# Attention sums with the values stationary and 512 columns moving, on one core of Trainium2

## The chip, the core and the metric

The kernel runs on one core of a Trainium2 chip. The metric is the device time of one execution in microseconds. It is taken as the median of several runs; for the kernel before it is 2655.85 us (three runs, 2655.58 to 2656.35).

## What is computed

All data are f32. An attention without softmax is followed by a mixture of experts in which a hash of the token's id picks the expert.

```
B, S, D = 8, 2496, 256;  K = 64                  # z is (B, S, K)
scores = (1/S) * z @ z.T                          # symmetric, per batch
x = u * (max(scores, 0)**2 @ v)                   # (B, S, D)
expert = token_ids * 2654435761 % 8               # per token
out[token] = max(x[token] @ w1[expert], 0) @ w2[expert]   # w1 256 x 1024, w2 1024 x 256
```

## The kernel before, in words

**Tiles and groups.** The 2496 tokens of a batch are 20 tiles (T): 19 of 128 and a last one, TM, of 64. Five groups (NG) of four tiles (G) are the queries; each group sums over all 20 tiles. The squared scores are symmetric, so for a group g only the tiles of later groups and its own are computed (`fresh`); those of earlier groups are obtained by turning blocks that were made before. All of the order is written out by hand; each engine executes its own instructions in exactly that order.

**Scores** (`scores`, line 206). One matmul per tile gives 128 keys by 512 queries in one bank of `mm_ps` (six banks). K is 64, so two matmuls share the array, by halves of its rows. ScalarE (ACT), and VectorE (DVE) for a few, writes the relu to a block `a` (pool `apool`, seven buffers of 4 tiles x 512). `square` (line 226) squares in place on ACT, two tiles per step of the main loop. In a group's own block only the part above the diagonal is computed, in most groups (`skipped`), and `own_turns` (line 258) turns small pieces in place.

**Turns** (`turns_of`, line 244). A block of group a with g > a is turned for group g by 16 DVE transposes, each of 32 partitions x 512, which write straight to the right quarter of a `mirror` buffer. `turn_scores` (line 283) issues some at each step, by a budget of ns; `turn_now` issues the rest where a user comes.

**Sums** (`attend`, line 333). For each tile and each of four query tiles, the 128 x 128 squares are the stationary operand and `v` (128 keys x 256) moves; the result, queries by 256, lies in two accumulators of two halves (`acc`). The last group has three whole query tiles and one of 64, which `attend_short` (line 305) sums by itself in a 64-column strip. `attend_last` adds the short tile TM, by halves of the rows.

**Gates** (`gate`, line 341). DVE multiplies `acc` by u and (1/S)^2 into `x_sb`. `place_x` (line 552) scatters each 128 rows of x to the token's slot in DRAM (`x_rows`), by an indirect DMA on GpSimd (POOL).

**Order of a group** (main loop, line 640). Two first tiles (EARLY) for half the queries, then for the other half; tiles 2 to 15, one per step; the short tile; then the scores of the next group; then the last three tiles (LATE) and the gates, half by half. After each step `square`, `turn_scores` and `between` add their work; `between` also spreads the sort of tokens by expert (`places`), the clearing of `x_rows` and the scatters. Loads of u, v and z stand on SyncE's (SP's) queue at the starts of groups.

**Experts** (`run`, line 763). Blocks of 512 slots and of 128 slots alternate. `ups` multiplies by w1 into `h_ps` and relus on ACT and DVE in turn; `down` multiplies by w2. `load_w`, `load_x` (both on SP) and `turn_x` (DVE) prepare the next blocks. Block 0 is loaded before the attention ends.

Of the kernel before, what the change touches and what calls it, by code (L numbers as in the profile page):

```python
# [24 lines left out]
def kernel(  # L25
# [10 lines left out]
    nc = tc.nc  # L36
# [29 lines left out]
    NS = -(-(NW * BLK // P + NP) // CLEAR) * CLEAR  # L66
    C = B * T
    c2 = (1.0 / S) ** 2
# [11 lines left out]
    NA = NG + 2  # L80
    apool = pool("apool", NA)
    xpool = pool("xpool", 3)

# [3 lines left out]


    slot_dram = nc.dram_tensor("slot_tokens", (P * NS,), I32)


    short = const.tile([P, T, R], F32)
    odd = const.tile([R, D], F32)
# [4 lines left out]
    nc.gpsimd.memset(short[R:P, TM, :], 0.0)  # L98
# [24 lines left out]
    zn, zT, v_sb, u_sb, x_sb, made, mirror, to_square, to_turn, gated = {}, {}, {}, {}, {}, {}, {}, [], [], []  # L123
# [24 lines left out]
    def load_v(b):  # L148
        v_sb[b] = vpool.tile([P, T, D], F32, name="v_sb")
        for g in range(NG):  # L150
            tiles_io(vf, b, group(g), v_sb[b][:, g * G:, :], False, nc.sync, twice=True)
# [21 lines left out]

    def whole(g):

        return range(G if g < NG - 1 else G - 1)

# [15 lines left out]
    def skipped(b, g, t):  # L193

        if t // G != g or b == 0 and not fine(g):
            return 0
        return (t % G if fine(g) else t % G // 2 * 2) * P

    def fine(g):


        return g > 1
# [3 lines left out]
    def scores(b, g):  # L206

        n = sum(width(t) for t in group(g))
        for k, t in enumerate(fresh(b, g)):
            lo = skipped(b, g, t)  # L210
# [15 lines left out]
    def square(n):  # L226
        for b, g, t in to_square[:n]:
            a = made[b, g, t // G][:, t % G, :]
            m = len(whole(g)) * P
            lo = skipped(b, g, t)  # L230
            pairs = [(a[:, lo:m], a[:, lo:m])] if lo < m else []
            if m < G * P:
                pairs.append((short[0:width(t), t, :], a[0:width(t), ds(m, R)]))
            for o, x in pairs:
                nc.scalar.square(o, x)  # L235
            if t % G == G - 1 and (t // G > g or b or fine(g)):
                turns = turns_of(b, g, t // G) if t // G > g else own_turns(b, g)
                to_turn.extend((n, (b, g, t // G), f) for n, f in turns)

                to_turn.sort(key=lambda e: min(e[1][2] - g, 2 if fine(g) else 1))  # L240
        del to_square[:n]


    def turns_of(b, a, g):

        def turn(r, c, m):
            if (b, a, g) not in mirror:
                mirror[b, a, g] = mirrors.pop(0)
            nc.vector.transpose(  # L249
# [586 lines left out]
```

## Time and profile before

| | before |
|---|---|
| median of three runs | 2655.85 us |
| profiled execution | 2659.45 us |
| its span, first to last instruction | 2657.6 us |
| TensorE busy | 2645.2 us (100%) |
| VectorE, ScalarE, GpSimd busy | 1394.4, 598.1, 495.9 us |
| attention sums, `acc` line 338, matmul instructions | 3472 + 2304 |
| first matmul of the experts starts | 1537.85 us |
| DMA | 274.44 MB |

The page shows one profiled execution. Engines are PE (TensorE's matmuls), PEld (its weight loads, which run beside PE), DVE, ACT, POOL and SP (SPq is its issuing of DMAs). An f32 matmul appears as two instructions. The ends of matmuls are modelled, so the interval from one start to the next tells TensorE's pace better than the duration. A group's line reads: line, engine, operation, out<-in, shapes, count | busy us, mean ns of one | idle time of the engine before it and what ended it. A timeline's line reads: start us, length us, engine, line, operation, count [idle before <- what released it]. L338 is line 338 of the kernel.

### The profile page before, as it was taken

Reading aid. Unit: us, or ns where it says so; the run is one execution under the profiler, and the core shown is the slowest. Engines: PE = TensorE matmul, PEld = TensorE weight load, DVE = VectorE, ACT = ScalarE, POOL = GpSimd, SP = SyncE. Lnnn points to the kernel's source line nnn. Section 1 sums busy time; section 2 is a strip of 40 time slices with the busy share of each in tenths; the row PEclk is TensorE's granted clock in tenths of the full one; section 3 lists DMA queues with packets and bytes.
Section 4 is the critical chain, followed back from the end, with each engine's and each line's share of the span. In section 5 each row is a group of like instructions: output and inputs, shape, how many; then the busy total and the mean of one; then the engine's idle time right before and its main releaser. Section 6 shows DMA issues by size and latency. Waiting matters only on the chain.

```text
span 2657.6 us, 32524 instructions
## 1 busy us (share of the span) xinstructions
PE 2645.2 (100%) x12054; PEld 2073.0 (78%) x12054; DVE 1394.4 (52%) x2907; ACT 598.1 (23%) x1304; POOL 495.9 (19%) x512
## 2 busy tenths in 40 slices
PE   9999999999999999999999999999999999999999
PEld 7787888888888888888878867777777777777777
DVE  7976887878878877887878811111111111111111
ACT  5115214223233133123142111111111111111111
POOL 1322122212221222222201111111111111111112
PEclk9999999999999999999999999999999999999999
DMA  8612212202210221122101276666666666666663
GB/s 294 202 32 71 37 32 70 51 18 70 51 59 29 51 71 37 34 69 52 33 16 32 63 182 166 158 159 153 156 158 156 155 156 164 165 165 163 165 157 84
DMA packets 306288, 274.44 MB, mean 103 GB/s; under 512 B 179116, under 2 KB 269117, under 8 KB 306128
## 3 DMA queue, kind: packets, MB, share of 16 engines
q1 hardware_dynamic: 285392, 231.25, 34.8%
q0 software_dynamic: 20736, 41.10, 4.8%
q8 instruction: 96, 1.57, 0.3%
q14 instruction: 64, 0.52, 0.1%
HBM read 208.91 MB, written 64.79 MB: 103 GB/s over the span
## 4 chain that ended last, share of the span: by engine, by line
PE 55%; issue 37%; POOL 6%; DVE 2%; POOLq 0%; DMA 0%; SPq 0%; ACT 0%
PE acc L338 45%; PE s_ps L213 7%; POOL out_dram L757 6%; PE acc L330 1%; PE q_ps L310 1%; DVE m L249 1%; POOLq L757 0%; PE warm L569 0%; POOL x_rows L555 0%; DMA v_sb<-x_rows 0%; DVE x_sb L347 0%; DMA x_rows<-x_sb,slot_i 0%; DVE slot L527 0%; DVE per_e L491 0%; SPq L614 0%
## 5 line engine op out<-in xcount | busy, mean ns | idle before, releaser
L249 DVE STREAM_TRANSPOSE m<-a 32x512 f32<-32x512 f32 (+1 forms) x1280 | 865.1, 676 | 21.5 <-ACT a L235 0.9
L338 PE MATMUL acc<-v_sb,a 128*128 128x256 f32 x3472 | 766.9, 381 | 2.2 <-issue 2.0
L338 PEld LDWEIGHTS acc<-v_sb,a 128*128 128x128 f32 x3472 | 656.9, 190 | 100.4 <-issue 10.0
L739 DVE TENSOR_SCALAR hT<-h_ps 128x512 f32<-128x512 f32 x161 | 111.4, 692 | 946.2 <-PE h_ps L733 924.2
L733 PE MATMUL h_ps<-v_sb,m 128*128 128x128 f32 (+1 forms) x2080 | 567.7, 431 | 1.4 <-PEq L797 1.4
L745 PE MATMUL o_ps<-m,hT 128*128 128x256 f32 x2576 | 566.3, 379 | 0.0
L745 PEld LDWEIGHTS o_ps<-m,hT 128*128 128x128 f32 x2576 | 486.9, 190 | 77.6 <-issue 14.3
L338 PE MATMUL acc<-v_sb,m 128*128 128x256 f32 x2304 | 504.6, 380 | 2.8 <-DVE x_sb L347 2.8
L733 PEld LDWEIGHTS h_ps<-v_sb,m 128*128 128x128 f32 x2080 | 317.6, 191 | 235.5 <-issue 230.6
L338 PEld LDWEIGHTS acc<-v_sb,m 128*128 128x128 f32 x2304 | 438.8, 191 | 63.6 <-DVE x_sb L347 3.6
L221 ACT ACTIVATE a<-s_ps 128x512 f32<-128x512 f32 (+3 forms) x456 | 205.4, 592 | 855.3 <-PE s_ps L213 855.3
L555 POOL DMA_INDIRECT x_rows<-x_sb,slot_i x160 | 156.2, 976 | 1067.8 <-DVE x_sb L347 883.6
L757 POOL DMA_INDIRECT out_dram<-o_sb,idx x157 | 153.5, 977 | 918.2 <-ACT o_sb L752 910.3
L235 ACT ACTIVATE a<-a 128x512 f32<-128x512 f32 (+3 forms) x472 | 232.8, 651 | 0.0
L265 DVE STREAM_TRANSPOSE a<-a 32x128 f32<-32x128 f32 (+1 forms) x992 | 221.6, 248 | 10.2 <-issue 1.1
L213 PE MATMUL s_ps<-zT 64*128 64x512 f32 (+1 forms) x960 | 195.0, 545 | 0.3 <-ACT zT L171 0.3
L752 ACT COPY o_sb<-o_ps 128x256 f32<-128x256 f32 x161 | 59.9, 372 | 595.4 <-PE o_ps L745 595.4
L737 ACT ACTIVATE hT<-h_ps 128x512 f32<-128x512 f32 x161 | 96.1, 597 | 368.7 <-PE h_ps L733 358.1
L213 PEld LDWEIGHTS s_ps<-zT 64*128 64x128 f32 x960 | 120.3, 186 | 71.2 <-issue 41.5
L543 POOL DMA_INDIRECT slot_tokens<-token,addr x160 | 156.1, 976 | 75.2 <-issue 50.4
L347 DVE SCALAR_TENSOR_TENSOR x_sb<-acc,u_sb 128x256 f32<-128x256 f32 x152 | 57.8, 420 | 194.7 <-PE acc L338 194.5
L633 DVE STREAM_TRANSPOSE v_sb<-v_sb 128x1024 f32<-128x1024 f32 (+1 forms) x65 | 53.9, 829 | 3.5 <-DMA v_sb<-x_rows 3.5
(101 smaller groups left out, 293.6 us busy)
## 6 DMA issues: line engine op xcount, KB each, us to landing
m<-in_moe_w_dram SPq DMA_DIRECT2D x260, 256.0 KB
m<-in_moe_w_dram SPq DMA_DIRECT2D x65, 1024.0 KB
x_rows<-zero SPq DMA_DIRECT2D x10, 2176.0 KB
v_sb<-in_v_dram SPq DMA_DIRECT2D x32, 512.0 KB
u_sb<-in_u_dram SPq DMA_DIRECT2D x32, 512.0 KB
v_sb<-x_rows SPq DMA_DIRECT2D x128, 128.0 KB
zn<-in_z_dram SPq DMA_DIRECT2D x28, 304.0 KB
v_sb<-x_rows SPq DMA_DIRECT2D x132, 32.0 KB
```

Source lines behind the costliest of these rows:

```text
L213: nc.tensor.matmul(ps[:, lo:n], zT[b][h, ts(t, P)], zT[b][h, ds(g * G * P + lo, n - lo)], start=True, stop=True)
L221: nc.scalar.activation(a, ps[:, lo:n], AF.Relu)
L235: nc.scalar.square(o, x)
L249: nc.vector.transpose(mirror[b, a, g][ts(c, Q)].rearrange("p t s q -> p (t s) q")[:, 0:m, ts(r, Q)], made[b, a, g][ts(r, Q)].rearrange("p ...
L265: return n * Q, lambda: nc.vector.transpose(out, in_)
L338: nc.tensor.matmul(acc[i // 2][:, i % 2, :], lhs(b, g, t, i), v_sb[b][:, t, :], start=(k == 0 and i % 2 == 0), stop=(k == TM - 1), skip_gr ...
L543: st = nc.gpsimd.indirect_dma_start(out=slot_dram[:, None], out_offset=bass.IndirectOffsetOnAxis(ap=addr[0:n, c:c + 1], axis=0), in_=token ...
L555: st = nc.gpsimd.indirect_dma_start(out=x_dram[:, :], out_offset=bass.IndirectOffsetOnAxis(ap=slot_i[0:width(c % T), c:c + 1], axis=0), in ...
L733: nc.tensor.matmul(ps[:, ts(i, n)], w1[j][:, c, ts(k * m + i, P)], xT[j][:, :, c, :], start=(c == 0), stop=(c == DP - 1))
L739: nc.vector.tensor_scalar_max(o, ps[:], 0.0)
L745: nc.tensor.matmul(ps[:], hT[j][f][:, ts(t, P)], w2[j][:, f, :], start=(f == 0), stop=(f == FP - 1))
L757: st = nc.gpsimd.indirect_dma_start(out=out[:], out_offset=bass.IndirectOffsetOnAxis(ap=rows, axis=0), in_=o, in_offset=None, bounds_check ...
```

## The change

The roles in the sums are swapped: 128 columns of v (every second one, `h::2`) are stationary and 512 squares move, so the result comes out turned, 128 columns of x by 512 queries, in one bank per half of v. The group's 448 queries of the last group move together, and `attend_short`, `short` and `odd` go. DVE turns a quarter of a block's columns on all 128 partitions at once into a `stage` buffer (pool `spool`, five); three DMAs on SP and one copy on ACT carry the quarters to the mirror. The factor 1/S moves into the square. The gate is now a DVE transpose of a bank; four DMAs take x to DRAM (`x_way`), one or two fetch it back some steps later in token order, and POOL multiplies by u. u is loaded at step 8 of its own group, v at five places of the batch before, z in group 3. `apool` has six buffers for seven. Only padding slots of `x_rows` are cleared. The own triangle is skipped in all groups. At the experts' start, `load_w` for the first partial block comes after the attention, and block 0's down comes ahead of that block's up.

```diff
-    NA = NG + 2
+    NA = NG + 1
...
+    qpool = pool("qpool", 2)
+    spool = pool("spool", 5)
...
+    x_way = [nc.dram_tensor(f"x_way_{k}", (G, NQ, Q, D), F32) for k in range(2)]
...
+    def queries(g):
+        return sum(width(t) for t in group(g))
...
+    def skipped(g, t):
+
+        return t % G * P if t // G == g else 0
...
+            a = made[b, g, t // G][:, t % G, skipped(g, t):queries(g)]
+            nc.scalar.activation(a, a, AF.Square, scale=1.0 / S)
...
     def turns_of(b, a, g):
...
+        key = b, a, g
+        def turn(c):
+            if key not in mirror:
+                mirror[key] = mirrors.pop(0)
+            stage = spool.tile([P, G * G * Q], F32, name="stage")
+            nc.vector.transpose(stage[:].rearrange("p (n q) -> p n q", q=Q),
+                                made[key][:].rearrange("p t (s q) -> p (t s) q", q=P)[:, :, ts(c, Q)])
+            for r in range(NQ):
+
+                m = len(group(g)) if r * Q < width(group(g)[-1]) else G - 1
+                o = mirror[key][ts(c, Q), 0:m, r].rearrange("p i s q -> p i (s q)")
+                x = stage[ts(r, Q), 0:m * G * Q].rearrange("p (i n) -> p i n", i=m)
+                if r == c:
+                    to_copy.append((key, lambda o=o, x=x: nc.scalar.copy(o, x)))
+                else:
+                    nc.sync.dma_start(o, x)
+        for c in range(NQ):
+            yield lambda c=c: turn(c)
...
     def turn_scores(steps):
...
+        nonlocal share
+        copy_turned(to_copy[:])
+        share += 1.2 * steps
+        own = [e for e in to_turn if e[0][1] == e[0][2]][:3]
+        others = [e for e in to_turn if e[0][1] < e[0][2]]
+        for e in own:
+            turn(e)
+        while share >= 1 and others and (mirrors or others[0][0] in mirror):
+            turn(others.pop(0))
+            share -= 1
+        share = min(share, 1)
...
+    def attend(b, g, k, acc, halves):
         t = summed(b, g)[k]
         turn_now((b, t // G, g))
-        for i in queries:
-            if i in whole(g):
-                nc.tensor.matmul(acc[i // 2][:, i % 2, :], lhs(b, g, t, i), v_sb[b][:, t, :],
-                                 start=(k == 0 and i % 2 == 0), stop=(k == TM - 1), skip_group_check=True)
+        for h in halves:
+            nc.tensor.matmul(acc[h][:, 0:queries(g)], v_sb[b][:, t, h::2], squares(b, g, t),
+                             start=(k == 0), stop=(k == TM - 1), skip_group_check=True)
...
+    def gate(b, g, h, acc):
+        n = queries(g) // Q
+        if h == 0:
+            x_q[b, g] = qpool.tile([P, G * NQ, D // NQ], F32, name="x_q")
+        x = x_q[b, g]
+        nc.vector.transpose(x[:, 0:n, h::2], acc[h][:, 0:n * Q].rearrange("p (n q) -> p n q", q=Q))
+        if h == 0:
             return
...
+        for a in range(NQ):
+            nc.sync.dma_start(o[:].rearrange("i j p d -> p (i j) d")[:, 0:n, ts(a, D // NQ)], x[ts(a, Q), 0:n])
+        m = len(whole(g))
+        def fetch():
+            nc.sync.dma_start(xs[:, 0:m], o[0:m].rearrange("i j p d -> (j p) i d"))
+            if m < G:
+                nc.sync.dma_start(xs[0:R, m], o[m, 0:R // Q].rearrange("j p d -> (j p) d"))
+            for k, t in enumerate(group(g)):
+                y = xs[0:width(t), k, :]
+                nc.gpsimd.tensor_mul(y, y, u_sb[b, g][0:width(t), k, :])
+                gated.append((b * T + t, y))
+        to_fetch.append((i + 3, fetch))
...
+    V_LOADS = [(4, 4), (1, 9), (2, 9), (3, 6), (3, 12)]
...
-        if g == 2 and b + 1 < B:
+        if g == 3 and b + 1 < B:
             load_z(b + 1)
...
+            if t == 8:
+                load_u(b, g)
+            if b + 1 < B and (g, t) in V_LOADS:
+                load_v(b + 1, V_LOADS.index((g, t)))
+            attend(b, g, t, acc, range(2))
...
+            attend(b, g, t, acc, [k])
+            gate(b, g, k, acc)
             square(2)
             turn_scores(1 if k else 0.8)
...
+            if first < i == AHEAD:
+
+                while do:
+                    do.pop(0)()
             up = ups(work[i]) if i < last else None
...
+    load_w(work[1], 1)
     load_x(work[1], 1)
```

## The prediction

> **What bounds the kernel now.** I read the busy shares by stage first, then TensorE's timeline, then the groups by shape, then the waits. By stage (columns: stretch; busy PE, PEld, DVE, ACT, POOL with counts; granted clock; DMA share; GB/s):
>
> ```profile
> core 0: us, PE busy (x) PEld busy (x) DVE busy (x) ACT busy (x) POOL busy (x), PEclk, DMA share, GB/s
> ...
> 100.00:140.00 40.00, 35.35 (x152) 28.15 (x150) 32.04 (x70) 2.88 (x8) 12.91 (x13) 0.91 0.37 73
> 175.00:365.00 190.00, 190.00 (x922) 158.26 (x923) 151.29 (x330) 54.95 (x124) 43.91 (x45) 1.00 0.18 49
> 365.00:554.00 189.00, 189.00 (x920) 157.39 (x918) 152.55 (x332) 54.05 (x122) 43.83 (x45) 1.00 0.18 49
> ```
>
> One batch takes 189.6 us (the chain of waits has the same 26.10 us piece of line 338 start at 364.62 and again at 554.23). In it TensorE is never idle, DVE is at 80%, ACT at 29%, DMA at 18%. So a lighter DVE is worth nothing by itself in seven of eight batches; only TensorE's own time counts. "Busy" could still hide slack, so I take start-to-start intervals from the timeline in the expert stage (each f32 matmul is two instructions):
>
> ```profile
> 2004.61 13.98 PE L745 MATMUL o_ps<-m,hT 128*128 128x256 f32 x64
> 2018.42 3.60 PE L733 MATMUL h_ps<-v_sb,m 128*128 128x512 f32 x8
> 2021.86 3.62 PE L745 MATMUL o_ps<-m,hT 128*128 128x256 f32 x16
> 2025.31 1.02 PE L733 MATMUL h_ps<-v_sb,m 128*128 128x512 f32 x2
> ```
>
> 256 columns: (2018.42-2004.61)/64 = 215.8 ns. 512 columns: (2021.86-2018.42)/8 = 430 ns. The wide form saves about 2 ns in 432. TensorE already streams columns without a gap, and the change leaves the number of columns nearly alone. This is the main fact of the case.
>
> The only idle TensorE time in the attention is in batch 0:
>
> ```profile
> 99.47 1.99 PE L338 MATMUL acc<-v_sb,m 128*128 128x256 f32 x8 [0.36 <-DVE x_sb L347]
> 103.94 14.04 PE L338 MATMUL acc<-v_sb,m 128*128 128x256 f32 x56 [2.48 <-DVE x_sb L347]
> ...
> 123.35 0.47 PE L338 MATMUL acc<-v_sb,a 128*128 128x256 f32 x1 [0.19 <-issue]
> 125.46 0.49 PE L338 MATMUL acc<-v_sb,a 128*128 128x256 f32 x1 [1.64 <-issue]
> 126.16 6.12 PE L338 MATMUL acc<-v_sb,a 128*128 128x256 f32 x20 [0.21 <-issue]
> ```
>
> 4.9 us in all, where the gates (line 347) stood behind turns and the sort on DVE; the clock of 0.91 over these 40 us is another 40 x 0.09 = 3.6 us. The groups that change:
>
> ```profile
> L249 DVE STREAM_TRANSPOSE m<-a 32x512 f32<-32x512 f32 x1024 | 719.1, 702 | 17.9 <-ACT a L235 0.9 <-issue 0.6
> L338 PEld LDWEIGHTS acc<-v_sb,a 128*128 128x128 f32 x3472 | 656.9, 190 | 100.4 <-issue 10.0
> L162 DVE STREAM_TRANSPOSE zT<-zn 128x512 f32<-128x512 f32 x35 | 24.1, 703 | 0.4
> ```
>
> A transpose of 128 partitions takes as long as one of 32.
>
> **The skill.** "TensorE: Matmul & The Clock Gate", section "Wait — 56ns, not 53.3ns?": warm, matmuls start N/2.4 GHz + 2.5 ns apart. With two columns' time per column of f32 that is 215.8 ns for 256, as measured, 429.2 for 512 (measured 430), and 375.8 for 448, which I use. Same page, "What's actually happening": the clock is halved or freed by windows of 3413 ns; the trace agrees in kind, since the slow stretches come just after the idle ones above. "SBUF — State Buffer", section "Door 1": lines of 16 bytes, strides up to 4 f32 cost nothing; the weights' new stride is 2, no run here shows one. "DMA: Bandwidth & Descriptors", section "Anatomy of one DMA": about 2 us fixed per DMA; it is told of GpSimd's path, and here SP's loads at 1542.5 were used at 1545.6, with eight issues between, which agrees.
>
> **Part by part.** Sums, TensorE, on the path. Before: 3472 + 2304 = 5776 instructions x 0.2158 = 1246.5 us, and the short-tile sums (line 310) from 1528.34 to line 330's start at 1532.80, 4.46 us x 8 = 35.7. After, per batch 4 groups x 19 tiles x 2 halves of 512 and 38 of 448, two instructions each: 2432 x 0.4292 + 608 x 0.3758 = 1272.3 us. Change -9.9 us. The last short tile (line 330) keeps its columns, four instructions of 512 for eight of 256: 0.
>
> Weights with stride 2: 190 ns now. If a stride doubled it, 380 still fits below the 429 ns of a matmul: 0. Only above 429 would it show, x 3040; I leave that to the tail, since the page says such a stride is free.
>
> Scores (line 213): the own triangle is now skipped in every group, 512 columns less per batch, 1536 in batch 0, 5120 in all. 39 instructions, nearly 9728 columns, took 8.25 us (775.31 to 783.56), 0.85 ns each: -4.3 us.
>
> DVE, per batch: 160 turns of 32 partitions go (865.1/8 = 108 us), 40 of 128 come (x 0.703 = 28), own turns rise by about 50 x 0.25 = 13, gates are 10 transposes of about 0.7 for 8 us of multiplies. 152 becomes about 84 of 188 us: off the path, except that the batch 0 idle should go: -4.9 - 3.6 = -8.5 us (bounds 0 and -8.5; the sort stays on DVE, but its backlog of 1280 turns is gone).
>
> What replaces the turns: per quarter-turn three 64 KB DMAs on SP and one ACT copy. SP issues take 0.30 to 0.49 us (line 614's least and middle). 120 turn DMAs x 0.49 = 59 us per batch, x out and back 26 x 0.49 = 13, z about 14, u and v 12 x 0.4 = 5: 91 of 188. The densest stretch is group 0, 1.2 quarters per step, 3.6 DMAs x 0.49 = 1.76 us against a step of 1.72, at the low price 1.1; 16 quarters have 19 steps, so SP is done in time either way. A stage buffer is held for 0.7 + 3 x 0.49 + 2 = 4.2 us, and five of them allow one quarter per 0.84 us. First use of a quarter is a group, 33 us, or at least ten steps later. Hidden behind TensorE: 0; without that cover each late quarter costs its lateness. ACT: 40 copies x 0.65 (the square's time) = 26 on top of 54: 80 of 189. POOL: 20 multiplies of 256 columns at 2.9 us/1280 = 0.6: 12 on top of 44.
>
> Moved loads: u to step 8 of its own group, v to five places, z from group 2 to 3, x by DRAM and back. All stand on SP in order, so a wait for a gate or for x's landing (about 2 us) holds the turn DMAs behind it; their ten steps cover it. The clearing of x_rows shrinks from ten DMAs of 2176 KB to pads: nothing waits on TensorE.
>
> Entry to the experts: x's longer way (gate, out 2+2, back 3, four multiplies 2.6, scatters 5 x 1.3, landing 2, load 3: about 22 us) is covered, as block 0's up (13.8) and down (13.8, now placed before the partial block's up) run first. But the next whole block's turn on DVE now stands behind the partial block's relu (0.69 + 1.24 + 0.2 = 2.1 us) and its matmuls follow at once: +2.1, or 3.8 with a half-clock window (1.7). The old order gave 13.8 us of cover. I take +3.
>
> Sum: -9.9 - 4.3 - 8.5 + 3 = -19.7 us. The profiled execution took 2659.45 (span 2657.6) and would take 2639.8; the median of the runs is 2655.85, so I forecast 2636.
>
> **The new waits, and the rivals.** On DVE the order of the built program puts, at two boundaries of each batch, a quarter-turn between the two gates of a group. The turn waits for ACT's fourth square of the next group, and gate 1 is queued behind; TensorE waits for gate 1 before its third matmul of the next group.
>
> ```profile
> 776.36 8.51 ACT L221 ACTIVATE a<-s_ps 128x512 f32<-128x512 f32 x18 [1.51 <-PE s_ps L213]
> 784.73 10.07 ACT L235 ACTIVATE a<-a 128x512 f32<-128x512 f32 x20
> ```
>
> On this clock: scores end 783.3, six matmuls of 0.75 end 787.8; relus end 784.5, squares are 0.52 apart, the fourth is done at 786.7, the turn at 787.4, gate 1 at 788.9; TensorE wants the bank at 789.5. It fits by 0.6 us. After group 0, counted from the first score: 7424 columns x 0.85 = 6.3, six matmuls of 0.86 to 11.5, bank wanted at 13.2; sixteen relus to 8.4, the fourth square done at 10.6, the turn at 11.3, gate 1 (bank complete 11.9) at 12.6: again 0.6.
>
> Rival A, slower (16%): ACT runs late there (copies ahead of the relus wait for DVE, DVE for stage buffers), so gate 1 is late by 1.6 us or more and the clock halves (1.7 more): 3.3 us at 23 boundaries (two per batch, and group 3's, where own turns stand between the gates) = 76, giving 2712. It turns the sign from 19.7/23 = 0.86 us per boundary. For: thin margin. Against: DVE and ACT half idle.
>
> Rival B (15%): batch 0's idle stays, since the sort still interleaves with gates: 2636 + 8.5 = 2644.
>
> Rival C (8%): small stalls at group starts, 0.4 us x 40 = 16, give 2652: no change to be told (0.2% is 5 us, about what a measurement of this kernel can tell).
>
> The forecast keeps 61%, own range 2628 to 2643. Faster 0.76 (forecast and B), same 0.07, slower 0.17 (A, 0.01 of C). The range runs from 2626 to 2656, where A alone is left out.
>
> **What would show it.** Right: 3040 sum instructions 429 ns apart, line 310's work gone, TensorE idle only after the partial block's up, batch period near 188 us, DVE near 45%. Wrong: TensorE waiting for a gate at group starts, half-clock windows in every batch, weight loads over 400 ns, or copies on ACT waiting for DVE ahead of the relus.

## The result, and the profile after

The kernel after takes 2676.75 us (median of four runs, 2674.95 to 2685.0); the kernel before took 2656.1 us beside it (four runs, 2655.58 to 2657.91). The ratio is 1.0083, with a 95% interval of 1.0070 to 1.0095: slower by 0.8%, against a forecast of 2636 us. The profiled execution of after is the slowest of its four, 2685.0 us with a span of 2683.3, so it is set against before's profiled 2659.45 (span 2657.6): +25.6 us.

First the busy shares of after by stage: the stretch of batch 0 that was shown of before, then batch 2, then batch 7.

```profile
core 0: us, PE busy (x) PEld busy (x) DVE busy (x) ACT busy (x) POOL busy (x), PEclk, DMA share, GB/s
100.00:140.00 40.00, 40.00 (x104) 18.29 (x103) 22.13 (x64) 15.00 (x32) 11.80 (x13) 1.00 0.57 137
391.50:584.80 193.30, 190.11 (x524) 89.81 (x522) 76.22 (x233) 78.18 (x158) 57.98 (x66) 1.00 0.47 113
1367.20:1560.00 192.80, 192.80 (x536) 92.09 (x533) 74.29 (x230) 77.85 (x158) 33.61 (x40) 1.00 0.45 107
```

In this stretch batch 0 lost its idle time. But batch 2 takes 193.3 us where before took 189.6, although VectorE (DVE) is busy for half as long, and TensorE now has 3.2 us idle. Measured from one batch's first score to the next one's, the two profiled executions differ like this:

| | before | after | change |
|---|---|---|---|
| up to the first score | 8.91 | 9.53 | +0.6 |
| batch 0 | 197.13 | 187.37 | -9.8 |
| batches 1 to 6 | 1137.7 (189.62 each) | 1170.6 | +32.9 |
| batch 7 | 194.12 | 192.60 | -1.5 |
| experts, from their first matmul | 1119.73 | 1123.22 | +3.5 |
| sum, the span | 2657.6 | 2683.3 | +25.7 |

The groups of the sums in after, by shape, and the waits of TensorE (PE) between 190 and 1550 us (us in total, times, longest):

```profile
L323 PE MATMUL acc<-a,v_sb 128*128 128x512 f32 (+1 forms) x1760 | 768.0, 593 | 0.0
L323 PE MATMUL acc<-m,v_sb 128*128 128x512 f32 (+1 forms) x1280 | 529.2, 571 | 5.5 <-DVE x_q L339 4.5
L323 PEld LDWEIGHTS acc<-a,v_sb 128*128 128x128 f32 x1760 | 343.0, 197 | 391.6 <-issue 374.7
```

```profile
PE s_ps L210 <- ACT a L218: 11.3, 8, 2.4
PE s_ps L210 <- issue: 5.1, 4, 2.0
PE acc L323 <- DVE x_q L339: 4.5, 6, 1.1
```

The sums themselves hardly wait: 1760 + 1280 = 3040 instructions, as forecast, and weights with a stride load in 197 ns (190 before). Undisturbed intervals are 0.429 us for 512 columns and 0.376 for 448. All 11.3 + 5.1 us of waiting for relus and "issue" belongs to the scores, line 210; in before no matmul of this stretch waits at all. So I looked at one boundary between groups, where scores are made. A relu is ScalarE's reading of one tile of scores, and the first one shows when ACT learns that the first scores are done. This is the boundary from group 0 to group 1 in batch 2 of before, TensorE and then ScalarE (ACT):

```profile
437.00 6.81 PE L213 MATMUL s_ps<-zT 64*128 64x512 f32 x32
```

```profile
438.06 7.52 ACT L221 ACTIVATE a<-s_ps 128x512 f32<-128x512 f32 x16 [22.49 <-PE s_ps L213]
```

And this is TensorE there in after (start us, length, operation, count, idle before):

```profile
432.97 2.74 PE L210 MATMUL s_ps<-zT 64*128 64x512 f32 x12
437.51 5.15 PE L210 MATMUL s_ps<-zT 64*128 64x512 f32 x20 [1.79 <-issue]
442.59 5.43 PE L323 MATMUL acc<-a,v_sb 128*128 128x512 f32 x12
```

and ACT at the same time:

```profile
430.12 0.51 ACT L249 COPY m<-stage 32x384 f32<-32x384 f32 x1 [1.40 <-DVE stage L241]
431.90 0.51 ACT L249 COPY m<-stage 32x384 f32<-32x384 f32 x1 [1.27 <-issue]
436.86 0.60 ACT L218 ACTIVATE a<-s_ps 128x512 f32<-128x512 f32 x1 [4.45 <-PE s_ps L210]
437.61 6.81 ACT L218 ACTIVATE a<-s_ps 128x512 f32<-128x512 f32 x15 [0.15 <-remote]
```

The first relu starts 436.86 - 432.97 = 3.89 us after the first score; in before it is 1.06 here and at the next two boundaries (0.95 for group 4; 1.48 at the start of a batch, where the first scores are mixed with the last sums). ACT was not busy: it had been idle for 4.45 us, waiting for line 210. The twelve scores filled the six banks and TensorE stopped for 1.79 us. In the trace's semaphore records, TensorE's first completion signal of this boundary stands at 436.84, 3.44 us after the start of the matmul that gives it (433.40); in before, at the same boundary, it comes 0.60 us after the start. The other held-up signals follow close behind; at this boundary in batch 1 all six stand 42 to 45 ns apart. So by their starts the scores were made in time, and what came late was the word that they were done.

From group 0 to 1 the first relu is late in each of batches 1 to 6 (4.14, 3.89, 4.51, 1.40, 4.14, 3.91 us after the score), in batch 7 it is not (1.05; the bursts of scatters there are of four and end before the boundary). From group 1 to 2 the signals are held up about 2 us into the scores; from group 3 to 4 a gate comes 1.0 to 1.3 us late. After a stop the scores go at the pace of the relus, and after five of the stops the granted clock is 0.50 for 3.4 or 6.8 us (242.9 to 246.3, for one; after the stop at 437.51 it stays at 1.00). For batches 1 to 6 this makes +43.3 us against six undisturbed batches of 187.88 us (which runs 5 and 8 below show): 35.0 in the scores (173.5 against 6 x 23.08) and 8.3 in the sums (968.65 against 6 x 160.06).

What else runs at that boundary? GpSimd (POOL) issues its scatters, x to the tokens' rows and slots to `slot_tokens`:

```profile
421.28 2.77 POOL L354 TENSOR_TENSOR x_sb<-x_sb,u_sb 128x256 f32<-128x256 f32 x4 [29.77 <-DMA m<-stage]
424.22 1.01 POOL L562 DMA_INDIRECT x_rows<-x_sb,slot_i  x1 [0.16 <-POOL x_sb L354]
...
434.42 0.98 POOL L550 DMA_INDIRECT slot_tokens<-token,addr  x1 [0.30 <-issue]
```

Nine scatters, 1.28 us apart, lie over the boundary at 432.97. In before they lay in the middle of a group, with boundaries at 437.00 and 477.71; the first and the last of its nine:

```profile
447.34 0.98 POOL L555 DMA_INDIRECT x_rows<-x_sb,slot_i  x1 [29.45 <-DVE x_sb L347]
...
457.62 0.98 POOL L543 DMA_INDIRECT slot_tokens<-token,addr  x1 [0.31 <-issue]
```

And SyncE's queue (SPq), with all its DMAs of line 251 in after (least, median, most ns) below:

```profile
406.01 2.24 SPq L346 DMA_DIRECT2D x_way<-x_q  x4
408.35 7.80 SPq L251 DMA_DIRECT2D m<-stage  x12
416.33 0.46 SPq L349 DMA_DIRECT2D x_sb<-x_way  x1
...
417.46 14.11 SPq L251 DMA_DIRECT2D m<-stage  x21
431.67 0.54 SPq L120 DMA_DIRECT2D u_sb<-in_u_dram  x1
```

```profile
L251 SPq DMA_DIRECT2D m<-stage x960: 3/599/1653, 20.6 to 1510.0; - x192
```

"Perfetto Trace Analysis", section "DMA Instruction — HWDGE (DVE, Sync)" of the Trainium skill, says what such a slice is: waiting for the descriptor generator, using it and pushing semaphores, not the movement of data. So 0.599 us is what a DMA of 64 KB costs SP's queue. At 3 x 1.2 = 3.6 of them per step that is 2.16 us, and a step takes 1.72: SP falls behind in groups 0 and 1, where it is issuing nine us of every ten in their second halves. x's way back, behind the turns, starts only at 416.33, 16.6 us ahead of the boundary (23.4 us in run 5 below, which has no turn DMAs), and its four products and the scatters follow from there. u leaves at 431.67, 1.3 us ahead of the boundary (22.4 us in run 5).

Three things thus meet at the boundary: the moved loads (u here, u and v at the next boundaries), the scatters, and the turn DMAs of SP. The experiments take them apart.

### The profile page after: what moved, and what is told of

Read it like the earlier page. It is cut to its first block, busy times and chain, and to the rows that moved or that the text cites. A ratio compares the mean times of both kernels' runs of the same rounds, so it can differ in the third digit from the quotient of the medians.

```text
span 2683.3 us, 28098 instructions
## 1 busy us (share of the span) xinstructions
PE 2652.4 (99%) x8854; PEld 1534.3 (57%) x8854; DVE 795.7 (30%) x2147; ACT 785.0 (29%) x1592; POOL 608.9 (23%) x671
## 5 line engine op out<-in xcount | busy, mean ns | idle before, releaser
L323 PE MATMUL acc<-a,v_sb 128*128 128x512 f32 (+1 forms) x1760 | 768.0, 593 | 0.0
L323 PEld LDWEIGHTS acc<-a,v_sb 128*128 128x128 f32 x1760 | 343.0, 197 | 391.6 <-issue 374.7
L323 PE MATMUL acc<-m,v_sb 128*128 128x512 f32 (+1 forms) x1280 | 529.2, 571 | 5.5 <-DVE x_q L339 4.5
L323 PEld LDWEIGHTS acc<-m,v_sb 128*128 128x128 f32 x1280 | 250.5, 196 | 279.8 <-issue 267.7
L354 POOL TENSOR_TENSOR x_sb<-x_sb,u_sb 128x256 f32<-128x256 f32 (+1 forms) x160 | 111.1, 723 | 989.0 <-DMA x_sb<-x_way 766.1
L262 DVE STREAM_TRANSPOSE a<-a 32x64 f32<-32x64 f32 (+3 forms) x1408 | 298.8, 241 | 20.0 <-ACT a L226 6.4
L249 ACT COPY m<-stage 32x512 f32<-32x512 f32 (+1 forms) x320 | 189.6, 593 | 300.9 <-DVE stage L241 139.7
L241 DVE STREAM_TRANSPOSE stage<-a 128x512 f32<-128x512 f32 x320 | 218.0, 700 | 200.8 <-DMA m<-stage 179.5
L226 ACT ACTIVATE a<-a 128x512 f32<-128x512 f32 (+1 forms) x480 | 236.9, 564 | 2.1
L210 PE MATMUL s_ps<-zT 64*128 64x512 f32 (+2 forms) x960 | 207.6, 555 | 16.7 <-ACT a L218 11.3
```

The lines of the kernel that those rows point to most:

```text
L210: nc.tensor.matmul(ps[:, lo:n], zT[b][h, ts(t, P)], zT[b][h, ds(g * G * P + lo, n - lo)], start=True, stop=True)
L226: nc.scalar.activation(a, a, AF.Square, scale=1.0 / S)
L241: nc.vector.transpose(stage[:].rearrange("p (n q) -> p n q", q=Q), made[key][:].rearrange("p t (s q) -> p (t s) q", q=P)[:, :, ts(c, Q)])
L249: to_copy.append((key, lambda o=o, x=x: nc.scalar.copy(o, x)))
L262: return lambda: nc.vector.transpose(out, in_)
L323: nc.tensor.matmul(acc[h][:, 0:queries(g)], v_sb[b][:, t, h::2], squares(b, g, t), start=(k == 0), stop=(k == TM - 1), skip_group_check=True)
```

## Experiments

The theories are named in the expectations as they stood then. Each ratio is against before's runs on the same chip.

### Run 1: the loads earlier

```diff
-    V_LOADS = [(4, 4), (1, 9), (2, 9), (3, 6), (3, 12)]
+    V_LOADS = [(4, 4), (1, 3), (2, 3), (3, 3), (3, 5)]
...
-            if t == 8:
+            if t == 2:
                 load_u(b, g)
```

> The changed kernel, with u loaded at step 2 of its group instead of step 8, and v's tiles at steps 3 and 5 instead of 9, 6 and 12. Theory (collision): SyncE issues a turn DMA every 0.60 us, falls behind, and issues u and v so late that they are in flight during the next group's scores; together with GpSimd's indirect DMAs they hold up TensorE's completion signals, so relus and gates start 1.5 to 3.5 us late. Then the first relu comes 1.06 us after the first score at every boundary, the batch period falls from about 194.5 to 190 us, and the time from about 2676 to 2650 us. Rival (order of ScalarE and VectorE: copies and turns ahead of the relus): no change, 2672 to 2680. Rival (the turn DMAs' 512-byte packets themselves hold up the signals): no change or worse.

Measured: 2691.91 us (2690.05 to 2697.55), ratio 1.013 (1.0116 to 1.0145). The loads were no longer at the scores, but the relus came late at both boundaries, 3.6 to 4.5 us after the first score from group 0 to 1 and 1.6 to 4.8 us from group 1 to 2, and batch 2 took 196.99 us. The turn DMAs were now issued up to 446.7, with the boundary at 435.2 and a burst of nine scatters from 425.7 to 436.8. The theory that the loads do it falls.

### Run 2: no scatters in batches 1 to 6

All rows of `x_rows` are cleared, and the scatters of x and of slots in batches 1 to 6 are left out, so most of the experts' input is missing.

```diff
-        c = NW * BLK // P + k * -(-NP // CLEAR)
-        n = min(NS - c, -(-NP // CLEAR))
+        n = -(-NS // CLEAR)
+        c = k * n
+        n = min(NS - c, n)
...
-        st = nc.gpsimd.indirect_dma_start(
+        if not 0 < c // T < 7:
+            st = nc.gpsimd.indirect_dma_start(
...
         c, x = gated.pop(0)
+        if 0 < c // T < 7:
+            return
```

> The changed kernel, leaving out GpSimd's indirect DMAs (the scatter of x and of the slot numbers) for batches 1 to 6, and clearing all of x_rows in batches 0 and 1 instead; so the experts get no rows of these batches. The loads of u and v stay where they are. Read batches 2 to 6 only. Theory (collision of loads with indirect DMAs): first relus at 1.06 us, batch period 188 to 190 us. Rival (the loads alone are enough): late first relus remain, period 192 to 195. Rival (order of ScalarE and VectorE): the same, 192 to 195.

Measured: 2670.15 us (2669.62 to 2670.44), ratio 1.0042 (1.0027 to 1.0056). The total is not to be used: the larger clearing disturbs batch 0, where relus wait up to 11 us. Batch 1 still has bursts of nine, with batch 0's tokens, and there a first relu is 3.75 us behind its score. In batches 2 to 6, which have no scatters, every first relu is 1.06 us behind (0.95 for group 4) and the period is 187.88 us, with the loads and the turn DMAs still at the scores. The scatters are needed for the loss; loads and turn DMAs without them do no harm.

### Run 3: before, with its loads moved to the scores

```diff
+            if k == 0 and (b or g):
+                load_u(b, g)
+                c, h = (b, g - 1) if g else (b - 1, NG - 1)
+                if c + 1 < B:
+                    load_v(c + 1, [h])
...
-        if n + 1 < len(groups):
-            load_u(*groups[n + 1])
-        if g == 0 and b + 1 < B:
-            load_v(b + 1)
```

> The kernel before, with the loads of u and of one fifth of v moved from the middle of a group to its scores: a one-element ScalarE copy into their buffers after the first relu holds them back to that point. Nothing of the turn DMAs is in it. Theory (collision): TensorE's completion signals come late at the boundaries that have indirect DMAs, TensorE idles there, 1 to 3 us a boundary, some 20 to 40 us more than before (2675 to 2695). Rival (the turn DMAs are needed for it): within 3 us of before.

Measured: 2660.78 us (13 runs) against 2658.42, ratio 1.0008 (1.0000 to 1.0016), and every first relu as in before. A batch takes 189.83 us for 189.62. 1 MB landing during the scores is all but harmless in before too. Its scatters stayed in mid-group, so this tests the loads alone.

### Run 4: the entry to the experts in the old order

```diff
-                if k == (1 if i + 1 > AHEAD else banks[-1]) and AHEAD <= i + 1 < max(last, loads):
+                if k == (0 if i == AHEAD else 1 if i + 1 > AHEAD else banks[-1]) and AHEAD <= i + 1 < max(last, loads):
                     turn_x(work[i + 1], (i + 1) % LOADS)
```

> The changed kernel, with the turn of the next whole block's x placed ahead of the partial block's relus on VectorE instead of behind them. The step of the sum at the entry to the experts (+2.1 for the wait, +1.7 for a half-clock window) says 3 to 3.8 us less than the changed kernel. If x's way by DRAM is what is late there, no change.

Measured: 2684.85 us (six runs, 2676.19 to 2692.62), ratio 1.0099 (1.0082 to 1.0116). The attention's late signals vary from run to run by more than the entry is worth, so the trace decides. TensorE at the entry in after, and then in run 4:

```profile
1587.62 3.73 PE L742 MATMUL h_ps<-v_sb,m 128*128 128x128 f32 x32
1593.29 5.40 PE L742 MATMUL h_ps<-v_sb,m 128*128 128x512 f32 x8 [1.94 <-DVE v_sb L644]
```

```profile
1575.44 13.98 PE L754 MATMUL o_ps<-m,hT 128*128 128x256 f32 x64
1589.26 7.17 PE L742 MATMUL h_ps<-v_sb,m 128*128 128x128 f32 x40
```

The stop of 1.94 us is gone, and the eight matmuls that took 5.40 us at half clock are no longer there. The expert stage takes 1119.3 us for 1123.2: 3.9 us.

### Run 5: no turn DMAs

The three DMAs of each quarter-turn are left out, so three quarters of each mirror keep zeros.

```diff
                 if r == c:
                     to_copy.append((key, lambda o=o, x=x: nc.scalar.copy(o, x)))
-                else:
-                    nc.sync.dma_start(o, x)
...
+    for m in mirrors:
+        nc.gpsimd.memset(m[:], 0.0)
```

> The changed kernel, leaving out the three SyncE DMAs of every quarter-turn, so that only a quarter of the turned squares is right (the buffers are set to zero at the start). GpSimd's indirect DMAs and the loads stay. The second run says that the indirect DMAs are needed for the late signals, the first and third that loads at the scores are not. Theory (turn DMAs and indirect DMAs together): first relus at 0.95 to 1.06 us at every boundary of batches 1 to 6, batch period 187.9 us. Rival (the indirect DMAs with anything that this kernel added, such as x's way through DRAM): late first relus remain, period above 190 us.

Measured: 2637.69 us (one run) against 2656.36. No idle time of TensorE between 190 and 1500 us, every first relu at 1.06. A batch of run 5:

```profile
570.10:758.00 187.90, 187.90 (x523) 89.77 (x522) 75.96 (x233) 77.86 (x158) 58.02 (x65) 1.00 0.28 76
```

This is the forecast, to 2 us. All matmuls, transposes, copies and gates of the change are still in it, so the loss of 2676.75 - 2637.69 = 39 us needs the turn DMAs. It does not say how: without them SP is not behind, and the scatters too had moved away from the boundary (406.9 to 418.1, with the boundary at 423.6).

### Run 6: only the slots' scatters

x's scatters are left out in batches 1 to 6, as in run 2; the slots' stay.

```diff
         c, x = gated.pop(0)
+        if 0 < c // T < 7:
+            return
         st = nc.gpsimd.indirect_dma_start(
```

> As the second run, but with the scatter of the slot numbers (4 bytes a row) kept in all batches, and only the scatter of x (1 KB a row) left out for batches 1 to 6. If every indirect DMA of GpSimd collides with the turn DMAs, whatever it carries: late relus in batches 1 to 5, where the slot scatters run, at about half the boundaries of the changed kernel, period 189 to 193. If it is x's data that collides: period 187.9.

Measured: 2665.49 us (one run), period 187.88 us from batch 2 on. The five scatters left in a burst ended some 3 us ahead of the boundary (628.4 to 634.5, boundary 637.4), so the run says nothing on which kind is at fault. Run 14 asks it again.

### Run 7: scatters only where there are no turn DMAs

All scatters are held for groups 3 and 4, where few or no turns are sent; the edit of run 4 is in it.

```diff
-        elif i % 4 == 0 and i < SORT + 4 * C:
+        elif g > 2:
             assert next(place, None) is None
-            enter((i - SORT) // 4)
-        elif gated:
+            if entered < C and i % 5 < 3:
+                enter(entered)
+                entered += 1
+            if gated:
+                place_x()
+        elif g == 0 and gated and gated[0][0] // T < b:
             place_x()
```

> The changed kernel, with both kinds of scatter issued only in groups 3 and 4 of a batch, which have few turn DMAs, and for the last group's x in the next group 0; and with the turn of x at the entry to the experts ahead of the relus. All of the work is done. Theory (turn DMAs and indirect DMAs together): late relus only where both still meet, batch period 188 to 189 us, attention shorter by 25 to 40 us than in the changed kernel, 2638 to 2648 us in all, faster than before. Rival (indirect DMAs with any transfer): as many late signals, only elsewhere, above 2655.

Measured: 2773.6 us (2765.59 to 2779.44), ratio 1.0436 (1.0418 to 1.0453): the expectation failed. All first relus are at 1.06 us, as hoped, but now TensorE stops inside the sums. A batch of run 7, and TensorE's largest wait over the whole run:

```profile
424.30:634.40 210.10, 196.58 (x522) 92.62 (x520) 76.23 (x233) 78.03 (x158) 56.94 (x64) 0.96 0.44 104
```

```profile
PE acc L323 <- issue: 73.0, 93, 3.0
```

Bursts of 15 to 23 scatters in a row stand over most of these stops, during which the starts of neighbouring matmuls lie 0.7, 1.4 or 2.1 us apart instead of 0.376; DVE is held too. "issue" means that the profile shows nothing that TensorE waited for. There is a second way, then, in which scatters delay other engines, with no turn DMA beside them; I found no cause for it.

### Run 8: x by ACT's queue

All work is done. x's DMAs, 26 per batch, are issued by ACT, out one step and back five steps after the gate, so SP's queue keeps the turns and loads; the edit of run 4 is in it.

```diff
-        for a in range(NQ):
-            nc.sync.dma_start(o[:].rearrange("i j p d -> p (i j) d")[:, 0:n, ts(a, D // NQ)], x[ts(a, Q), 0:n])
+        def send():
+            for a in range(NQ):
+                nc.scalar.dma_start(o[:].rearrange("i j p d -> p (i j) d")[:, 0:n, ts(a, D // NQ)], x[ts(a, Q), 0:n])
...
-            nc.sync.dma_start(xs[:, 0:m], o[0:m].rearrange("i j p d -> (j p) i d"))
+            nc.scalar.dma_start(xs[:, 0:m], o[0:m].rearrange("i j p d -> (j p) i d"))
...
-        to_fetch.append((i + 3, fetch))
+        to_fetch.append((i + 1, send))
+        to_fetch.append((i + 5, fetch))
```

> The changed kernel, with x's way out to DRAM and back issued by ScalarE's DMA queue (one step after the gate, back four steps later) instead of SyncE's, so that neither a wait for the gate nor the turn DMAs stand before it, and with the turn of x at the entry to the experts ahead of the relus (3.9 us less there, by the trace of the fourth run). GpSimd's scatters then come in the middle of a group as in the kernel before, and not over its end. All of the work is done. Theory (scatters that fall on a group's boundary make TensorE's completion signals late, whatever else runs): first relus at 1.06 us, batch period 188 to 189 us, 2634 to 2645 us in all, faster than before. Rival (turn DMAs and scatters together, wherever they meet, cost TensorE time): 2655 or more.

Measured: 2635.85 us (2634.80 to 2636.67) against 2654.5, ratio 0.9929 (0.9916 to 0.9943): faster than both kernels. Batch 2 of run 8, then its boundary on TensorE, on ACT and on POOL:

```profile
382.50:570.40 187.90, 187.90 (x522) 89.75 (x520) 76.36 (x233) 78.27 (x158) 58.20 (x66) 1.00 0.50 116
```

```profile
423.84 6.60 PE L210 MATMUL s_ps<-zT 64*128 64x512 f32 x32
```

```profile
424.90 5.49 ACT L218 ACTIVATE a<-s_ps 128x512 f32<-128x512 f32 x11 [3.69 <-PE s_ps L210]
```

```profile
409.65 2.78 POOL L355 TENSOR_TENSOR x_sb<-x_sb,u_sb 128x256 f32<-128x256 f32 x4 [26.93 <-DMA x_sb<-x_way]
...
422.80 0.98 POOL L552 DMA_INDIRECT slot_tokens<-token,addr  x1 [0.31 <-issue]
```

The same operations as in after, the DMA share even higher (0.50), and no stop: 32 scores in one piece, the relu 1.06 us behind, though ACT has been idle ahead of it here too. Counted from the boundary, x's products start only 2.5 us sooner than in after (423.84 - 409.65 = 14.2 us ahead of the first score, for 432.97 - 421.28 = 11.7), but that is enough to issue the last of the nine scatters just before the first score. The turn DMAs still run over the boundary. At the next one, 464.16, a burst of nine does lie over it (454.4 to 465.7), with eight turn DMAs issued in its first half, and nothing is late there either.

### Run 9: before, with its scatters held to the scores

A small copy on POOL waits for the first relu of the next group, and the nine scatters follow it.

```diff
             to_square.append((b, g, t))
+            if k == 0 and held:
+                nc.gpsimd.tensor_copy(once_seen[:], a[0:1, 0:1])
+                release()
...
-            enter((i - 2 * T) // 4)
-        elif gated:
-            place_x()
+            held.append(lambda c=(i - 2 * T) // 4: enter(c))
+        elif len(gated) > len(later):
+            held.append(place_x)
+            later.append(0)
```

> The kernel before, with all the scatters of a group held back until the first relu of the next group: a one-element GpSimd copy of that relu's output stands ahead of them, so a burst of nine begins about 1.2 us after the first score. No turn DMA is in it. Theory (a burst at the boundary is enough): TensorE's signals come late in the scores, and TensorE idles 1.5 to 5 us at most boundaries, 50 to 150 us more than before. Rival (the turn DMAs are needed): within 5 us of before.

Measured: 2654.35 us (12 runs) against 2654.5, ratio 1.0000 (0.9991 to 1.0008). A burst of nine at the boundary is free in before. The theory that the burst is enough falls.

### Run 10: no turn DMAs, scatters held to the scores

The edit of run 9 on the kernel of run 5, so the turned data are missing again.

```diff
-            enter((i - SORT) // 4)
-        elif gated:
-            place_x()
+            held.append(lambda c=(i - SORT) // 4: enter(c))
+        elif len(gated) > len(later):
+            held.append(place_x)
+            later.append(0)
```

> As the fifth run (three SyncE DMAs of every quarter-turn left out, GpSimd's indirect DMAs kept), with the scatters held back to the first relu of the next group as in the run before this one. It has the changed kernel's burst at the boundary, and no turn DMAs. Theory (a burst at the boundary is enough): late signals and idle TensorE at most boundaries, above 2665 us. Rival (the turn DMAs are needed): 2636 to 2642 us as in the fifth run.

Measured: 2639.27 us (one run), period 187.88 us. The burst starts 2.5 us after the first score, as in run 11 below, where turn DMAs run too and it does harm. Here it does none.

### Run 11: run 8 with its scatters held to the scores

The edit of run 10, on the kernel of run 8: all work is done, only the scatters' place changes.

```diff
+            if k == 0 and held:
+                nc.gpsimd.tensor_copy(once_seen[:], a[0:1, 0:1])
+                release()
```

> The eighth run (x's way on ScalarE's DMA queue), with the scatters of a group held back to the first relu of the next group's scores as in the ninth and tenth. All of the work is done; turn DMAs and a burst of scatters now meet at the boundaries after groups 0 and 1. Theory (turn DMAs and scatters together at a boundary): late relus or idle TensorE there again, 2650 to 2680 us. Rival (it also takes x's transfers on SyncE's queue, or a SyncE that is behind): 2634 to 2642 us, as the eighth run.

Measured: 2666.51 us (2663.22 to 2669.45), ratio 1.0044 (1.0027 to 1.0061). TensorE's largest wait between 190 and 1550 us in run 11:

```profile
PE acc L326 <- DVE x_q L342: 18.6, 11, 2.8
```

The burst can start only after the first relu, so the relus are in time; the gates, a few us later, are now the late ones. The period of batch 2 is 193.1 us for 187.88. Few turn DMAs are enough: from batch 1 to 2 the burst runs from 388.5 to 399.8, only three turn DMAs are issued in it, from 398.4 on, and the second gate is late and stops TensorE for 1.69 us. Putting the burst back over a boundary with turn DMAs brings the loss back, in the version that had none: together they cost, and run 8's gain is one of place.

### Run 12: run 8 with x on SP's queue

```diff
-                nc.scalar.dma_start(o[:].rearrange("i j p d -> p (i j) d")[:, 0:n, ts(a, D // NQ)], x[ts(a, Q), 0:n])
+                nc.sync.dma_start(o[:].rearrange("i j p d -> p (i j) d")[:, 0:n, ts(a, D // NQ)], x[ts(a, Q), 0:n])
...
-            nc.scalar.dma_start(xs[:, 0:m], o[0:m].rearrange("i j p d -> (j p) i d"))
+            nc.sync.dma_start(xs[:, 0:m], o[0:m].rearrange("i j p d -> (j p) i d"))
```

> The eighth run with x's transfers back on SyncE's queue, but still sent one step after the gate and fetched four steps later, instead of at the gate and three steps later. If what the changed kernel suffers from is only the place in SyncE's order (turn DMAs that stand behind a wait for the gate): 2634 to 2645 us. If it is that SyncE has too much to issue (0.60 us a turn DMA) so that x comes back late in the group and the scatters fall on its end: 2655 to 2680 us, scatters at the boundary.

Measured: 2678.81 us (2677.22 to 2679.58), ratio 1.0086 (1.0069 to 1.0103), period of batch 2 194.4 us. TensorE over the boundary at 433.09, and the first and last of the scatters there:

```profile
433.09 4.71 PE L210 MATMUL s_ps<-zT 64*128 64x512 f32 x20
439.81 5.84 PE L210 MATMUL s_ps<-zT 64*128 64x512 f32 x12 [2.02 <-issue]
```

```profile
427.26 1.01 POOL L564 DMA_INDIRECT x_rows<-x_sb,slot_i  x1 [0.16 <-POOL x_sb L355]
...
437.45 0.98 POOL L552 DMA_INDIRECT slot_tokens<-token,addr  x1 [0.30 <-issue]
```

Fourteen turn DMAs are issued during this burst. At the next boundary, 479.96, the burst (475.2 to 486.5) meets only four, all before the first score, and nothing stops. So it is not the later steps for x that help in run 8 but the other queue: on SP, x stands behind the turns wherever the program puts it.

### Runs 13 and 14: one kind of scatter at the scores

Run 11 with the slots' scatters left out in batches 1 to 6, and run 11 with x's left out there, by the edits of run 2 (run 14 clears all rows again).

```diff
+        if not 0 < c // T < 7:
+            st = nc.gpsimd.indirect_dma_start(
```

> The eleventh run (x's way on ScalarE's DMA queue, scatters held to the next group's first relu), leaving out most scatters of slot numbers (those of tokens of batches 1 to 6), so that a burst at the boundary is four scatters of x alone; the experts then get few of the rows. If x's scatters with the turn DMAs are enough: gates and relus late at boundaries of batches 2 to 6 as in the eleventh run, period above 190.5 us. If the slot scatters are needed: 187.9 us.

```diff
         c, x = gated.pop(0)
+        if 0 < c // T < 7:
+            return
```

> The eleventh run, leaving out the scatter of x for batches 1 to 6 (and clearing all of x_rows instead, in batches 0 and 1), so that a burst at the boundary is some five scatters of slot numbers alone. If slot scatters with the turn DMAs are enough: late gates or relus in batches 2 to 5, period above 190.5 us. If x's scatters are needed: 187.9 us.

Measured: 2642.98 and 2661.81 us (one run each; the larger clearing disturbs batch 0 of run 14). From batch 2 on the period is 187.88 us in both, with no late relu or gate. Batch 1 still has bursts of nine, with batch 0's tokens, and gates are late there (TensorE stops for 1.57 and 2.51 us in run 13, for 1.63 in run 14). Neither kind does it alone: a burst of four or five beside turn DMAs is free, one of nine is not. Number and mixture change together here; nine of one kind were not tried.

### Run 15: before with DMAs beside its scatters

Run 9's kernel, with three DMAs within the on-chip memory for each quarter, into a buffer that nothing reads.

```diff
+            if r == c:
+                for s in range(NQ):
+                    if s != r:
+                        nc.sync.dma_start(waste[ts(c, Q)], made[b, a, g][ts(s, Q), :, ts(c, P)])
```

> The ninth run (the kernel before with the scatters held to the next group's first relu, which cost nothing), with three SyncE DMAs of 64 KB in 512-byte pieces from SBUF to SBUF added for every quarter of a block that VectorE turns, like the changed kernel's turn DMAs, into a tile that nobody reads. Theory (turn DMAs and scatters together are enough, whatever else the change brought): TensorE idles at boundaries, 20 to 80 us more than the ninth run (2675 to 2735). Rival (something else of the changed kernel is needed too): within 6 us of the ninth run.

Measured: 3025.16 us (3019.80 to 3029.51), ratio 1.1388 (1.1369 to 1.1407). Inconclusive: the added DMAs read `a`, and relus waited 217.6 us for them to release it. A delay of signals can't be told apart in that.

## Why the prediction was wrong

**What held.** The sums: 160.06 us per batch for 161.29, x 8 = -9.8 us (forecast -9.9). The stride of the weights: nothing to speak of, as the Trainium skill's "SBUF — State Buffer", section "Door 1", had it (197 ns of load for 190, under 429 of matmul). The scores: 23.08 us per batch for 23.70, and line 331 +0.11, so (-0.62 + 0.11) x 8 = -4.1 us (-4.3). An undisturbed batch takes 187.88 us for 189.62 (forecast "near 188"). Batch 0: -9.76 us, of which 9.76 - 1.74 = 8.0 beyond the faster batch (-8.5), so rival B didn't come. DVE is at 76 us per batch (84), ACT at 78 (80), POOL at 58 (56). The entry: +3.9 us by run 4 (+3), and by the mechanism named. The fit of 0.6 us at two boundaries held: in runs 5 and 8 no gate is late. Together -9.8 - 4.1 - 8.0 + 3.9 = -18.0 us, for the -19.7 of the forecast. From before's profiled 2659.45 that gives 2641.4; after's profiled execution took 2685.0, and the 43.3 us of batches 1 to 6 fill the gap to 0.3.

**Read wrongly, with little effect.** Of the 4.9 us of idle time in batch 0, only 0.36 + 2.48 = 2.84 stand behind gates; the lines of the other 2.04 say "issue". Those belong to the one profiled execution: in run 9, with before's sums, they are not there, and batch 0 takes 192.74 us, not 197.13. So the batch 0 term came close partly by luck. And the load that was used at 1545.6 did not have eight issues between, since the eighth starts at 1545.79; the trace there shows some 2 to 3 us from issue to use, and no more than that.

**The step that failed** is "What replaces the turns", with its "Hidden behind TensorE: 0" and "SP is done in time either way". It has two parts.

First, the price. I took 0.30 to 0.49 us for an issue from line 614, and it is 0.599. The trace of before has no DMA within the on-chip memory, and so no price for one, but it has a dearer row, which I used for z alone, the 28 loads from line 146 (least, median, most ns):

```profile
L146 SPq DMA_DIRECT2D zn<-in_z_dram x28: 587/598/665, 104.4 to 1257.7; - x28
```

With 0.6 the dense stretch is 3.6 x 0.6 = 2.16 us against a step of 1.72, and SP falls behind in it. The turn DMAs are 72 us per batch, not 59, and all of SP's issuing about 102, not 91.

Second, the consequence. I asked only whether the quarters are in time for the sums, and they are. Under "Moved loads" I asked what x's wait does to the turns behind it. I did not follow the other direction, what stands behind the turns on SP's queue: x's way back, hence POOL's products, hence the burst of nine scatters, which slid onto the boundary (without turn DMAs, in run 5, it ends 5.5 us ahead of it). There it ran beside the turn DMAs, and completion signals of TensorE reached ACT and DVE up to 3.5 us late. That the slide comes from the higher price, and would not have come at 0.49 us, no run shows. The runs show: no loss without the turn DMAs (5, 10), without the burst (2), with a burst of four or five (13, 14), with a burst of nine in before (9), or with the loads moved in before (3); loss with both at a boundary (after, 1, 11, 12), though not at each such boundary (one of run 8 and one of run 12 show none). What I had taken as hidden cost 2676.75 - 2637.69 = 39 us, nearly all of the 40.75 between result and forecast.

**The rivals.** Rival A had the side and the place, relus and gates at boundaries, but not the mechanism or the size. It had ACT behind copies that wait for DVE; ACT was idle for 4.45 us ahead of the late relu. It forecast 76 us (2712), and some 40 came. Rival C's small stalls are not there in runs 5 and 8.

**What stays open.** What it is that the two kinds of DMA share so that signals come late was not found. The nearest the trace has: SP's own issues show as slices under 0.1 us (held up, and then recorded in no time) 23 times in after, each within 3.3 us of the start of a burst's last scatter; in runs 8 and 11 none do, and run 11 still loses, so this doesn't explain it. Why run 8 is free, with one burst that ends as the scores begin and another over a boundary, is seen but not explained, and so are the stops of run 7. From group 3 to 4 in after, where gates are late and TensorE waits 4.5 us in all, the burst lies over the boundary too, but the turn DMAs beside it have just ended; runs 5 and 10 have no such wait. And what the turn DMAs hold up in the signals was shown by leaving them out, not by adding them to before: run 15, which tried that, was inconclusive.

## What to carry to other kernels

When a change puts many small DMAs of a new shape on a queue, price an issue by the queue's dearest row as well as by a cheap one, multiply by the densest step, and if the queue falls behind at either price, list what stands behind it and to where each of these slides. A queue that "is done in time" for its own users can still push another engine's bursts onto the place where every engine waits for signals. Moving the transfers that others wait for to a second queue turned +0.9% (run 12) into -0.7% (run 8) with the same work.

## What the runs showed of the hardware that I had not expected

- A DMA of 64 KB from 32 partitions to 32 others costs 0.599 us of the issuing queue, about as much as a load of z of 304 KB (0.598), and more than the median of 0.487 for the experts' loads of x from line 614. The Trainium skill's "DMA: Bandwidth & Descriptors", section "Issuing engines are not separate DMA queues", says that a second issuing engine saves only the time to initiate, "usually small relative to the DMA itself". Summed up it was not small here: 102 of 193 us in batch 2 of after were issuing on SP. And where the issues stood mattered more than their time: runs 8 and 12 differ by some 41 us (-18.7 and +22.8 us against before on the same chip) for 26 DMAs per batch. That the two queues share the same DMA engines, no run here shows.
- Nine scatters in a row with turn DMAs issued beside them, 14 or 15 or as few as three, made TensorE's signals up to 3.5 us late at a boundary of after, and show nothing at one boundary of run 8 and one of run 12. Nine without turn DMAs, or four or five with them, show nothing (runs 9, 10, 13, 14).
- While 15 to 23 scatters stood in a row, matmuls of the sums started 0.7, 1.4 or 2.1 us apart instead of 0.376, even without turn DMAs (run 7: 73.0 us in 93 stops).
- 1 MB of loads landing during the scores costs about 0.2 us per batch in run 3 (189.83 for 189.62) and nothing in run 2 (187.88, as in run 5).
